# Folding w_out beside the logits, w2 of seven experts by row halves, and a reordered tail, in an attention and two-MoE kernel on one core

## The chip, the core and the metric

The kernel runs on one NeuronCore of a Trainium2 chip. The core has TensorE (matmuls; "PE" in the profile, its weight loads "PEld"), VectorE ("DVE"), ScalarE ("ACT"), GpSimd ("POOL"), SyncE ("SP", which here issues every DMA), and 16 DMA engines. TensorE's array can be split into strips of 32 columns or 32 rows: an operation whose output has 32 rows of PSUM uses one column strip (column group), and the profile writes its shape as 128*32. The metric is the device time of one execution in microseconds (us). Lower is better.

## What is computed

```python
x = local_global_attention(q_l, k_l, v_l, q_g, k_g, v_g)   # 2304 tokens, 512 features
silu = g * sigmoid(g);  g = x @ w_gate;  val = x @ w_val    # d_ff = 1536
x = (silu * val) @ w_out                                    # w_out: 1536 x 512

# soft MoE on that x: 32 slots, 8 experts with 4 slots each
logits = x @ phi                                            # 512 x 32
d = softmax(logits, axis=0);  c = softmax(logits, axis=1)
slot_input = (d.T @ x).reshape(8, 4, 512)
for e in range(8):
    slot_out[e] = relu(slot_input[e] @ w1[e]) @ w2[e]       # 512 x 1024, 1024 x 512
out = c @ slot_out                                          # 2304 x 512
```

The kernel never forms the second x. It uses logits = h @ (w_out @ phi), with h = silu * val, and puts w_out into the slot inputs at the end.

## The kernel before

The program is written in order by hand, and each engine runs its own instructions in that order. Instructions of one engine are never reordered by a scheduler.

**Attention** comes first (16 units). It leaves x transposed in 18 tiles of 128 tokens, kept in five blocks: blocks 0, 1, 2 (512 columns each) are the group G1, blocks 3 (384 columns, `BA`) and 4 (256 columns, `BB`) are G2.

**First MoE.** d_ff is cut into `NFC` = 12 chunks of 128. For G1 and each chunk c, `gate` and `val` run on each of the three blocks: 12 matmuls each (`mm3`, line 598: 4 pieces of the contraction, each as three products of rounded and remainder parts). ACT then takes tanh of the gate, DVE multiplies twice (lines 613 and 622) and transposes into `hT`. G2 does the same afterwards with weights fetched again from DRAM.

Between the matmuls other work is inserted by a hand-written plan. A step is one quarter of a `gate` or `val` (3 matmuls); `at(k, f)` runs f after step k. A chunk of G1 is `S1` = 24 steps and a chunk of G2 is `S2` = 16. In G1 that work is, for each chunk:

- `wprime(c)` makes wp[c] = w_out[chunk] @ phi (128 x 32) in three parts. Part a (step +9) transposes w_out on TensorE (`pwt`) and ACT copies it (`woT`). Part b (step +12), the fold, has four matmuls (`pwp`, line 642), one for each quarter of the 512 features, each in its own column strip; DVE copies the four partial sums (`ws`). Part e (step +15) adds the four with one matmul against a stack of four identities (`pws`, line 651), and ACT copies the result to `wp`.
- `logits_piece(0, [c - 1])` (step +5, line 669) adds chunk c-1's part of the logits: three matmuls, one for each block, in column strips 0, 1 and 2 of the tile `L`. They read the `u` tiles of chunk c-1. There are two pools of `u` tiles, for even and odd chunks, with three tiles each, so the tanh of chunk c+1 can write only when chunk c-1's tile has been read.

**Slot inputs.** `sums` (line 760) adds exp(logits).T @ h for a block in 32x32 tiles. For block `BA` it runs in three calls during the end of G2, and after the last of them `last_expert` issues the DMA of the last w1 (`ha`, 2 MB), which overwrites that block's `hT`. The steps here are counted from k = `begin(10, BB)`.

**Experts.** w2 of an expert is 1024 x 512 (2 MB) and is loaded in two halves of 1 MB. `w2_load` has two ways. A half by rows is a run of 8 KB for each partition and holds half of the contraction for all columns. A half by columns holds the whole contraction for 256 output columns, in runs of 1 KB. `order2` says which way and in what order: experts 0 to 5 by rows, then columns 0 to 255 of experts 6 and 7, then columns 256 to 511 of experts 6 and 7. `expert2(e, a)` (line 1194) adds expert e's part to output half a: 8 matmuls in four column strips, into `pso[a]`.

**Tail.** `slots_out(a)` copies `pso[a]` (ACT), spreads it with one matmul (`ps4`) and copies it again (DVE). `tiles_out(a, kk)` multiplies by c for 8, 8 and 2 tiles of tokens, copies the results out of PSUM (ACT and DVE in turn) and issues the output DMAs: 9 for each half of the columns, most of them of 256 KB.

An fp32 matmul shows as two records in the profile.

Of the kernel before, what the change touches and what calls it, by code (L numbers as in the profile page):

```python
# [23 lines left out]
NC = DM // P  # L24
# [21 lines left out]
def attention_moe_soft_moe_kernel(  # L46
# [15 lines left out]
    nc = tc.nc  # L62
    FF = w_gate.shape[1]
    NFC = FF // P
    NS = phi.shape[1]
    E, _, F2 = w1.shape
# [18 lines left out]
    istack = cpool.tile([P, NS], F32, name="istack")  # L85
# [3 lines left out]
    phi_sb = cpool.tile([P, NC, NS], F32, name="phi_sb")  # L89
# [4 lines left out]
    for i, (_, n) in enumerate(BLOCKS):  # L94
        pool = x2pool if i in GROUPS[-1] else x1pool
        t = pool.tile([P, 2 * NC * n * P], F32R, name=f"x{i}")
        t = t.rearrange("p (a c n) -> p a c n", a=2, c=NC)
# [169 lines left out]
    pw = ps_sc.tile([P, 512], F32, tag="sc", name="pw")  # L267
# [21 lines left out]
    for g in (0, 1, 3, 2):  # L289
# [7 lines left out]
        for r in range(3):  # L297
# [3 lines left out]
            k = window(first)[1]  # L301
# [283 lines left out]
    def at(k, f):  # L585
        plan.setdefault(k, []).append(f)
# [40 lines left out]
    def wprime(c):  # L627

        d = {}

        def a():
            pt = ps_w.tile([P, NC, P], F32, tag="wt", name=f"pwt{c}")
            for cc in range(NC):
                nc.tensor.transpose(pt[:, cc], wo[c][:, cc * P : cc * P + P], ident)
            wo.pop(c)
            t = d["t"] = wtmp.tile([P, NC, P], F32, tag="woT", name=f"woT{c}")
            nc.scalar.activation(t, pt, AF.Copy)  # L637

        def b():
            pp = ps_w.tile([P, P], F32, tag="wp", name=f"pwp{c}")  # L640
            for j in range(NC):
                nc.tensor.matmul(
                    pp[32 * j : 32 * j + 32], phi_sb[:, j], d["t"][:, j],
                    start=True, stop=True, skip_group_check=True,
                )
            d["s"] = wtmp.tile([P, P], F32, tag="ws", name=f"ws{c}")
            nc.vector.tensor_copy(d["s"], pp)

        def e():
            pw = ps_w.tile([P, NS], F32, tag="wp", name=f"pws{c}")  # L650
            nc.tensor.matmul(pw, d["s"], istack, start=True, stop=True)
            nc.scalar.activation(wp[c], pw, AF.Copy)

        return a, b, e

    def logits_piece(g, cs, blks=None):

        group = GROUPS[g]
        per = 4 // len(group)

        def f():
            if g not in Lps:
                Lps[g] = ps_L.tile([P, 512], F32, tag="L", name=f"L{g}")
            for c in cs:
                for bi, blk in enumerate(group):
                    if blk not in (blks or group):
                        continue
                    cg, n = bi * per + c % per, cols(blk)
                    nc.tensor.matmul(  # L669
                        Lps[g][32 * cg : 32 * cg + 32, :n], wp[c], us.pop((c, blk))[:, :n],  # L670
                        start=(c < per), stop=(c >= NFC - per), skip_group_check=True,
                    )

        return f
# [171 lines left out]
    S1, S2 = 2 * NC * len(G1), 2 * NC * len(G2)  # L846
    for c in range(NFC):

        if c > 0:
            at(S1 * c + 5, logits_piece(0, [c - 1]))  # L850
        for k, f in zip((9, 12, 15), wprime(c)):
            at(S1 * c + k + (5 if c == 0 else 0), f)
        if c + 2 >= NFC:
            w_fetch(c + 2)
        for bi, blk in enumerate(G1):
            if c + 1 < NFC:
                w_prep(3 * (c + 1) + bi)
            if c > 0:
                gate(0, c, blk)
            prep_some(2)  # L860
            val(0, c, blk)
            prep_some(3)
# [33 lines left out]

    HD = DM // 2
    w1s, w2h, slots = {}, {}, {}
    NWHOLE = E - 2
    order2 = [(e, a, True) for e in range(NWHOLE) for a in range(2)]  # L900
    order2 += [(e, a, False) for a in range(2) for e in range(NWHOLE, E)]

# [7 lines left out]
    t = epool[0].tile([P, 4096], F32, name="dr0", tag="e0")  # L910
    t = [t[:, 512 * k : 512 * k + 512] for k in range(5)]
    d0, a, b, top, turned, tokens, sums, NJ = part_end(0, t[0], (t[1], t[0], t[1]), t[2:])
# [16 lines left out]
    k = base + 30  # L929
# [25 lines left out]
    def first_done():  # L955

        t = place["x"] = x2pool.tile([P, 8 * cols(BA)], F32, name="xa", tag=f"x{BA}")
        w2_load(0, t)
        o = 8 * cols(BA) - cols(BB)
        place["rB"] = t[:, o:]  # L960
        Ls, r = t[:, o - 2 * cols(BA) : o - cols(BA)], t[:, o - cols(BA) : o]
        d, a, b, top, turned, tokens, sums, NJ = part_end(1, Ls, [Ls], [r])

        al = []

        def spread():
            b()
            top(0)
            al.append(weights(0))

        def merge(i):
            nc.vector.scalar_tensor_tensor(
                out=Ts[:, i], in0=d["T"][i][:, 0:NF], scalar=al[0][:, 1:2], in1=Ts[:, i],
                op0=ALU.mult, op1=ALU.add,
            )

        def aside(i):
            t = upools[1].tile([P, 512], F32, tag="u", name=f"TA{i}", bufs=3)
            nc.scalar.activation(t[:, :NF], d["T"][i][:, 0:NF], AF.Copy, scale=al[0][:, 1:2])
            place["T", i] = t[:, :NF]  # L980

        def last_expert():

            place["h"] = h2pool.tile([P, NFC * cols(BA)], F32, name="ha", tag=f"h{BA}")
            w1_load(E - 1, place["h"][:, 0:4096])

        place["merge"] = merge
        k = begin(10, BB)
        at(begin(9, BB) + 3, a)
        at(begin(9, BB) + 6, spread)  # L990
        at(k + 1, lambda: turned(0))
        at(k + 3, lambda: nc.scalar.activation(Ts, Ts, AF.Copy, scale=al[0][:, 0:1]))
        at(k + 5, tokens)
        at(k + 6, lambda: weighted(0, al[0], ds[:, 2, 0:1]))
        for i, j in enumerate(range(0, NJ, 4)):
            at(k + 7 + 2 * i, sums(j, min(j + 4, NJ)))
        at(k + 12, last_expert)
        for i in (2, 3):
            at(k + 10 + i, lambda i=i: aside(i))

    wot = []

# [6 lines left out]
    for c, blk in order:  # L1009
        if blk == BA:  # L1010
            i = NFC + c
# [23 lines left out]
    d, a, b, top, turned, tokens, sums, NJ = part_end(2, Ls, [Ls], [place["rB"]])  # L1035
# [43 lines left out]
    t = dpool.tile([P, 4 * NF], F32, tag="Ts", name="sT")  # L1079
    nc.gpsimd.memset(t[:, : 5 * E * DG], 0.0)  # L1080
    t = t[:, : 5 * E * DG].rearrange("p (c k) -> p c k", c=5)
# [6 lines left out]
    for c in range(NFC):  # L1088
        cg = c % 4
        for h, hs in enumerate((H1, H2)):  # L1090
            nc.tensor.matmul(
                psi[h][32 * cg : 32 * cg + 32], TT[:, c], wot[c // 4][:, c % 4, hs],
                start=(c < 4), stop=(c >= NFC - 4), skip_group_check=True,
# [5 lines left out]
    for c in range(NC):  # L1099
        nc.tensor.matmul(  # L1100
            psTi[:, c], si[c // 2][:, c % 2 * P : c % 2 * P + P], istack,
            start=True, stop=True, skip_group_check=True,
# [88 lines left out]
    def expert2(e, a):  # L1191
        for f in range(NF2):
            j = f % 4
            nc.tensor.matmul(  # L1194
                pso[a][32 * j : 32 * j + 32], hx[f][:, NS * e : NS * e + NS], w2h[e, a, f],
                start=(e == 0 and f < 4), stop=(e == E - 1 and f >= 4), skip_group_check=True,
            )

    def slots_out(a, beside=()):

        sb = upools[1].tile([P, HD], F32, tag="u", name=f"psb{a}", bufs=3)
        nc.scalar.activation(sb, pso[a], AF.Copy)
        for f in beside:
            f()
        ps4 = psT.tile([P, DM], F32, tag="t", name=f"ps4{a}")
        nc.tensor.matmul(ps4[:, :HD], rep4, sb, start=True, stop=True)
        nc.vector.tensor_copy(s4[:, a], ps4[:, :HD])
# [3 lines left out]
    def tiles_out(a, kk):  # L1211
        n, qs = (2, range(4)) if kk < 2 else (1, [3])
        po = {q: psT.tile([P, 2, HD], F32, tag="t", name=f"po{a}_{kk}_{q}") for q in qs}
        for i in range(n):
            for q in qs:
                r = slice(32 * q, 32 * q + 32)
                nc.tensor.matmul(  # L1217
                    po[q][:, i], cT[r, 2 * kk + i], s4[r, a],
                    start=True, stop=True, skip_group_check=True,
                )  # L1220
        cs = slice(a * HD, a * HD + HD)
        for q in qs:
            o = ob[nob[0] % len(ob)]
            nob[0] += 1
            if q % 2 == 0:
                nc.scalar.activation(o[:, :n], po[q][:, :n], AF.Copy)
            else:
                nc.vector.tensor_copy(o[:, :n], po[q][:, :n])
            if kk < 2:
                rs = slice(G + 2 * P * kk, G + 2 * P * kk + 2 * P)  # L1230
                nc.sync.dma_start(out_b[q, rs, cs].rearrange("(i p) f -> p i f", p=P), o)
            else:
                nc.sync.dma_start(out_b[:, 0:G, cs], o[:, 0])

    for e in range(E):
        expert2(e, 0)
    slots_out(0, [lambda: expert2(0, 1)])
    for e in range(1, E):
        expert2(e, 1)
        if e <= 3:  # L1240
            tiles_out(0, e - 1)
    slots_out(1)
    for kk in range(3):
        tiles_out(1, kk)
# [58 lines left out]
```

## Time and profile before

| | |
|---|---|
| Median of 3 runs | 533.63 us (532.14 to 534.77) |
| The profiled execution's own time | 531.98 us |
| Its span, first to last instruction | 529.6 us |
| Mean granted TensorE clock | 0.987 |
| TensorE busy | 494.8 us, 93% of the span |
| VectorE busy | 303.7 us, 57% |
| ScalarE busy | 182.2 us, 34% |
| Bytes moved by DMA | 109.93 MB, mean 208 GB/s |

The span is what the trace covers; the execution's own time has 2.4 us around it. The chain that ended last is 68% TensorE, 12% "issue" (the engine waited for nothing that the profile shows), 8% ScalarE and 7% DMA. The stretches of the trace are: attention to about 111 us, G1 from there to 346 us, G2 to 457 us, the end of the slot inputs to 471 us, expert first layers to 485 us, expert second layers and the output to the end. Busy shares are averages over these; a saving counts only where the stage is bound by what is saved.

### The profile page before, as it was taken

Reading aid. Unit: us, or ns where it says so; the run is one execution under the profiler, and the core shown is the slowest. Engines: PE = TensorE matmul, PEld = TensorE weight load, DVE = VectorE, ACT = ScalarE, POOL = GpSimd, SP = SyncE. Lnnn points to the kernel's source line nnn. Section 1 sums busy time; section 2 is a strip of 40 time slices with the busy share of each in tenths; the row PEclk is TensorE's granted clock in tenths of the full one; section 3 lists DMA queues with packets and bytes.
Section 4 is the critical chain, followed back from the end, with each engine's and each line's share of the span. In section 5 each row is a group of like instructions: output and inputs, shape, how many; then the busy total and the mean of one; then the engine's idle time right before and its main releaser. Section 6 shows DMA issues by size and latency. Waiting matters only on the chain.

```text
span 529.6 us, 12507 instructions
## 1 busy us (share of the span) xinstructions
PE 494.8 (93%) x5110; PEld 369.1 (70%) x5110; DVE 303.7 (57%) x801; ACT 182.2 (34%) x550; POOL 97.1 (18%) x137
## 2 busy tenths in 40 slices
PE   7779999999999999999999999999999999989592
PEld 4567888887777677777677777786599998434241
DVE  7558888767776667677677667353233434550022
ACT  5849898963323223223223223111111112210011
POOL 7854465421201001001001001000000000010000
PEclk9999999999999999999999999999999999999897
DMA  8997696503653444444444463223099996899965
GB/s 208 278 293 230 206 271 172 167 11 100 219 178 124 158 157 156 143 139 160 139 141 159 140 228 125 85 94 147 2 366 400 410 414 210 298 420 419 359 201 179
DMA packets 51169, 109.93 MB, mean 208 GB/s; under 512 B 3752, under 2 KB 35496, under 8 KB 47656
## 3 DMA queue, kind: packets, MB, share of 16 engines
q1 hardware_dynamic: 51112, 109.13, 61.0%
q8 instruction: 40, 0.66, 0.5%
q14 instruction: 17, 0.14, 0.1%
HBM read 88.93 MB, written 20.19 MB: 206 GB/s over the span
## 4 chain that ended last, share of the span: by engine, by line
PE 68%; issue 12%; ACT 8%; DMA 7%; DVE 3%; SPq 0%; DVEq 0%; ACTq 0%
PE pval L598 23%; PE pgate L598 22%; DMA f<-in_w_dram 4%; PE sc L342 4%; ACT p L363 3%; PE T L760 3%; PE o L386 3%; PE ppT L372 2%; DMA fw<-in_w_dram 2%; PE pso L1194 2%; PE L L669 2%; ACT woT L637 1%; PE po L1217 1%; DMA qT<-in_qT_dram 1%; PE gs L447 1%
## 5 line engine op out<-in xcount | busy, mean ns | idle before, releaser
L598 PE MATMUL pval<-x,w 128*128 128x512 f32 x432 | 112.2, 400 | 0.0
L598 PE MATMUL pgate<-x,w 128*128 128x512 f32 x432 | 109.7, 398 | 0.0
L598 PEld LDWEIGHTS pval<-x,w 128*128 128x128 f32 x432 | 79.3, 188 | 28.2 <-issue 11.6
L598 PEld LDWEIGHTS pgate<-x,w 128*128 128x128 f32 x432 | 79.4, 189 | 16.6
L613 DVE SCALAR_TENSOR_TENSOR u<-u,pgate 128x512 f32<-128x512 f32 (+2 forms) x60 | 36.4, 607 | 84.6 <-ACT u L612 84.5
L612 ACT ACTIVATE u<-pgate 128x512 f32<-128x512 f32 (+2 forms) x60 | 31.8, 530 | 128.1 <-PE pgate L598 106.3
L622 DVE SCALAR_TENSOR_TENSOR u<-u,pval 128x512 f32<-128x512 f32 (+2 forms) x60 | 36.4, 607 | 48.6 <-PE pval L598 48.5
L172 POOL TENSOR_TENSOR w<-wb,w 128x512 fp32r<-128x512 f32 x24 | 31.2, 1302 | 179.9 <-ACT w L171 179.8
L363 ACT ACTIVATE p<-sm,nm 128x128 f32<-128x128 f32 x128 | 49.4, 395 | 0.0
L598 PE MATMUL pgate<-x,wr 128*128 128x384 f32 (+1 forms) x288 | 49.3, 314 | 0.0
L598 PEld LDWEIGHTS pgate<-x,wr 128*128 128x128 f32 x288 | 43.5, 188 | 8.1 <-issue 7.4
L598 PE MATMUL pval<-x,wr 128*128 128x384 f32 (+1 forms) x288 | 48.4, 313 | 0.0
L598 PEld LDWEIGHTS pval<-x,wr 128*128 128x128 f32 x288 | 43.1, 188 | 7.0 <-issue 7.0
L171 ACT ACTIVATE w<-wb 128x512 fp32r<-128x512 f32 x24 | 15.2, 632 | 86.7 <-issue 51.3
L342 PE MATMUL sc<-kS,qB 128*64 128x128 f32 x512 | 35.3, 286 | 7.9 <-ACT pG L466 3.3
L342 PEld LDWEIGHTS sc<-kS,qB 128*64 128x64 f32 x512 | 29.5, 142 | 13.6 <-issue 8.5
L353 DVE CUSTOM_DVE_ANT_0 sm<-sc,masks 128x128 f32<-128x128 f32 x128 | 28.9, 287 | 10.6 <-PE sc L342 8.9
L157 DVE SCALAR_TENSOR_TENSOR wb<-wv,wb 128x512 f32<-128x512 f32 x36 | 25.2, 700 | 3.5
L1080 POOL MEMSET sT<- 128x1440 f32 x1 | 1.3, 1297 | 138.5 <-PE U L1055 138.5
L625 DVE STREAM_TRANSPOSE hT<-u 128x512 f32<-128x512 f32 x36 | 25.6, 712 | 1.3
L143 DVE SCALAR_TENSOR_TENSOR wb<-raw,wb 128x512 uint32<-128x512 uint32 x36 | 24.9, 692 | 1.1
L363 ACT ACTIVATION_READ_ACCUMULATOR p<-sm,nm 128x1 f32 x128 | 24.9, 195 | 0.0
(207 smaller groups left out, 667.8 us busy)
## 6 DMA issues: line engine op xcount, KB each, us to landing
e<-in_w_dram SPq DMA_DIRECT2D x7, 2048.0 KB, 12.4
w_d<-w SPq DMA_DIRECT2D x24, 512.0 KB, 2.6
wr<-w_d SPq DMA_DIRECT2D x12, 1024.0 KB, 6.1
f<-in_w_dram SPq DMA_DIRECT2D x10, 1024.0 KB, 14.7
raw<-in_wgate_dram SPq DMA_DIRECT2D x12, 512.0 KB, 3.5
raw<-in_wval_dram SPq DMA_DIRECT2D x12, 512.0 KB, 4.0
raw<-in_wout_dram SPq DMA_DIRECT2D x12, 512.0 KB, 3.5
kS<-in_kS_dram SPq DMA_DIRECT2D x7, 736.0 KB, 7.2
```

The source lines that it names most:

```text
L143: nc.vector.scalar_tensor_tensor(out=d["t"], in0=d["raw"][:, :, 0], scalar=29, in1=d["t"], op0=ALU.logical_shift_right, op1=ALU.bitwise_or,)
L157: nc.vector.scalar_tensor_tensor(out=w, in0=d["v"], scalar=F64_NORMAL, in1=w, op0=ALU.is_ge, op1=ALU.mult)
L172: nc.gpsimd.tensor_tensor(out=wl, in0=w, in1=wh, op=ALU.subtract)
L342: nc.tensor.matmul(sc[64 * (i % 2) : 64 * (i % 2) + 64, i // 2], qb[:, hp, blk], kS[n][:, hp, 32 * s0 : 32 * s0 + 128], start=True, stop=T ...
L353: nc.vector.tensor_tensor_reduce(out=sm[:, bp], in0=sc[:, bp], in1=masks[:, 4 * tp + bp], scale=-SCALE, scalar=3e38, op0=ALU.add, op1=ALU.min,
L363: nc.scalar.activation(d["p"][hp][:, bp], d["sm"][hp][:, bp], AF.Exp, bias=d["nm"][:, hp, bp : bp + 1], scale=-1.0, accum_out=d["rs"][:, b ...
L386: nc.tensor.matmul(o[32 * g : 32 * g + 32, bp, hp], d["pT", hp][:, bp, 32 * g : 32 * g + 32], vW[n % 2][k][:, m, 2 * h2 + hp], start=True, ...
L598: nc.tensor.matmul(ps[:, :n], w[:, 2 * k + a, cc * P : cc * P + P], xt[b][:, cc], start=(cc == 0 and i == 0), stop=(cc == NC - 1 and i == 2),)
L612: nc.scalar.activation(u[:, :n], pg[:, :n], AF.Tanh, scale=0.5)
L613: nc.vector.scalar_tensor_tensor(out=u[:, :n], in0=u[:, :n], scalar=1.0, in1=pg[:, :n], op0=ALU.add, op1=ALU.mult)
L622: nc.vector.scalar_tensor_tensor(out=u[:, :n], in0=u[:, :n], scalar=0.5, in1=pv[:, :n], op0=ALU.mult, op1=ALU.mult)
L625: nc.vector.transpose(out=hT[blk][:, c], in_=u[:, :n])
```

## The change

There are three edits.

**Fold.** Part a of `wprime` stays at step +9 (+14 for chunk 0). The four matmuls of part b now all write to one column strip, rows 96 to 127 of PSUM, and add up there, instead of to four strips. The copy takes 32 rows, and part e contracts over 32 rows instead of 128. Part b of chunk c moves to step +3 of the next chunk (step +13 of the same chunk for chunk 11) and is put right behind `logits_piece(0, [c - 1])`, which moves there from step +5 of chunk c, so it is 22 steps later for chunks up to 9. Part e follows 6 steps after part b, which is the step of the next chunk's part a.

**Slot sums.** The three `sums` calls of block `BA` move from steps k+7, k+9, k+11 to k+6, k+7, k+8; `last_expert` from k+12 to k+9; two copies (`aside`) from k+12, k+13 to k+10, k+11.

**Tail.** w2 of expert 6 is loaded by rows, so that only expert 7 is loaded by column halves. The order of `expert2` mixes second halves into the first halves. All of `tiles_out(0, ...)` comes behind `expert2(7, 1)`, and `slots_out(1)` behind that.

```diff
         def b():
+            r = slice(3 * NS, 4 * NS)
             pp = ps_w.tile([P, P], F32, tag="wp", name=f"pwp{c}")
             for j in range(NC):
                 nc.tensor.matmul(
-                    pp[32 * j : 32 * j + 32], phi_sb[:, j], d["t"][:, j],
-                    start=True, stop=True, skip_group_check=True,
+                    pp[r], phi_sb[:, j], d["t"][:, j],
+                    start=(j == 0), stop=(j == NC - 1), skip_group_check=True,
                 )
             d["s"] = wtmp.tile([P, P], F32, tag="ws", name=f"ws{c}")
-            nc.vector.tensor_copy(d["s"], pp)
+            nc.vector.tensor_copy(d["s"][r], pp[r])

         def e():
+            r = slice(3 * NS, 4 * NS)
             pw = ps_w.tile([P, NS], F32, tag="wp", name=f"pws{c}")
-            nc.tensor.matmul(pw, d["s"], istack, start=True, stop=True)
+            nc.tensor.matmul(pw, d["s"][r], istack[r], start=True, stop=True)
             nc.scalar.activation(wp[c], pw, AF.Copy)
...
+        last = c == NFC - 1
+        f, fold, back = wprime(c)
+        at(S1 * c + (14 if c == 0 else 9), f)
+        k = S1 * c + 13 if last else S1 * (c + 1) + 3
         if c > 0:
-            at(S1 * c + 5, logits_piece(0, [c - 1]))
-        for k, f in zip((9, 12, 15), wprime(c)):
-            at(S1 * c + k + (5 if c == 0 else 0), f)
+            at(k, logits_piece(0, [c - 1]))
+        at(k, fold)
+        at(k + 6, back)
...
-    NWHOLE = E - 2
+    NWHOLE = E - 1
...
         for i, j in enumerate(range(0, NJ, 4)):
-            at(k + 7 + 2 * i, sums(j, min(j + 4, NJ)))
-        at(k + 12, last_expert)
+            at(k + 6 + i, sums(j, min(j + 4, NJ)))
+        at(k + 9, last_expert)
         for i in (2, 3):
-            at(k + 10 + i, lambda i=i: aside(i))
+            at(k + 8 + i, lambda i=i: aside(i))
...
-    for e in range(E):
-        expert2(e, 0)
-    slots_out(0, [lambda: expert2(0, 1)])
-    for e in range(1, E):
-        expert2(e, 1)
-        if e <= 3:
-            tiles_out(0, e - 1)
+    for e, a in ((0, 0), (1, 0), (2, 0), (3, 0), (4, 0), (0, 1), (1, 1), (5, 0), (2, 1), (3, 1),
+                 (6, 0), (4, 1), (5, 1), (7, 0)):
+        expert2(e, a)
+    slots_out(0, [lambda: expert2(6, 1)])
+    expert2(7, 1)
+    for kk in range(3):
+        tiles_out(0, kk)
     slots_out(1)
```

## Rows read from the trace of the kernel before

**Rows 1.** Windows: stretch, length, busy us per engine (instructions), clock, DMA share, GB/s.

```profile
150.00:321.00 171.00, 169.36 (x816) 125.53 (x815) 118.13 (x194) 46.30 (x89) 23.21 (x18) 1.00 0.47 158
```

**Rows 2.** Timeline of TensorE in one chunk of G1: start, us, what.

```profile
210.64 2.95 PE L598 MATMUL pgate<-x,w 128*128 128x512 f32 x12
213.43 1.54 PE L598 MATMUL pval<-x,w 128*128 128x512 f32 x6
214.90 1.06 PE L669 MATMUL L<-u,wp 128*32 128x512 f32 x6
215.89 1.66 PE L598 MATMUL pval<-x,w 128*128 128x512 f32 x6
...
220.62 0.86 PE L598 MATMUL pval<-x,w 128*128 128x512 f32 x3
221.64 0.43 PE L642 MATMUL pwp<-woT,phi_sb 128*32 128x128 f32 x8 [0.16 <-ACT woT L637]
222.00 2.35 PE L598 MATMUL pval<-x,w 128*128 128x512 f32 x9
224.19 0.34 PE L651 MATMUL pws<-istack,ws 128*128 128x32 f32 x2
```

**Rows 3.** The tile woT over the whole trace: who waited for it (us, times).

```profile
  PEld pwp L642: 6.1, 10
```

**Rows 4.** Windows of the end, same columns as Rows 1.

```profile
454.00:458.00 4.00, 4.00 (x53) 2.35 (x52) 1.30 (x4) 1.43 (x3) 0.00 (x0) 1.00 0.44 124
458.00:492.00 34.00, 30.37 (x383) 13.94 (x382) 11.54 (x27) 4.35 (x10) 2.05 (x2) 1.00 1.01 420
492.00:504.00 12.00, 5.89 (x66) 2.11 (x64) 0.00 (x0) 0.38 (x1) 0.00 (x0) 0.77 1.08 349
506.00:508.50 2.50, 2.50 (x46) 1.15 (x34) 0.88 (x2) 0.93 (x2) 0.00 (x0) 1.00 0.00 1
509.00:515.00 6.00, 6.00 (x95) 3.08 (x90) 1.71 (x3) 1.09 (x2) 0.00 (x0) 1.00 1.01 330
516.00:518.50 2.50, 1.87 (x20) 1.09 (x18) 0.89 (x2) 0.50 (x2) 0.00 (x0) 1.00 0.20 57
```

**Rows 5.** Timeline of the DMA issues on SyncE: start, us, what.

```profile
455.63 0.38 SPq L906 DMA_DIRECT2D ha<-in_w_dram  x1
...
508.20 5.04 SPq L1231 DMA_DIRECT2D out_dram<-ob  x8
...
518.62 4.30 SPq L1231 DMA_DIRECT2D out_dram<-ob  x7
```

**Rows 6.** Timeline of TensorE in the tail.

```profile
497.68 0.42 PE L1194 MATMUL pso<-f,hb 128*32 128x256 f32 x3 [2.37 <-DMA f<-in_w_dram]
...
506.41 1.15 PE L1217 MATMUL po<-s,xa 32*128 32x256 f32 x16
```

**Rows 7.** The chain of work that ended last, in the tail.

```profile
500.70 3.64 PE pso L1194 x32
...
505.48 1.00 PE pso L1194 x16
```

**Rows 8.** Timeline of TensorE, 458 to 470 us.

```profile
459.27 1.98 PE L1027 MATMUL idle<-e,ident 128*128 128x512 f32 x4
...
466.16 2.85 PE L1091 MATMUL psi<-wo,TT 128*32 128x256 f32 x48 [0.68 <-DVE w L785]
```

**Rows 9.** The chain of work that ended last, in G2.

```profile
354.06 1.43 PE pval L598 x12
```

**Rows 10.** Timeline of TensorE around the slot sums of block BA.

```profile
450.95 0.94 PE L760 MATMUL T<-h,xa 32*32 32x384 f32 x32 [0.46 <-DVE Lr L742]
451.82 0.98 PE L598 MATMUL pgate<-x,wr 128*128 128x256 f32 x6
452.74 0.93 PE L760 MATMUL T<-h,xa 32*32 32x384 f32 x32
```

**Rows 11.** The page's costliest groups: busy us, mean ns | idle before, what ended it.

```profile
L613 DVE SCALAR_TENSOR_TENSOR u<-u,pgate 128x512 f32<-128x512 f32 (+2 forms) x60 | 36.4, 607 | 84.6 <-ACT u L612 84.5
```

## The prediction

> **What bounds the kernel now.** I read the profile stage by stage, since the three edits fall into three stages. First come the windows of the middle of G1: TensorE is busy 169.4 of 171 us there, VectorE 118.1, and the DMA engines at less than half [rows 1]. So in G1 whatever TensorE executes beside the gate and val matmuls, or waits for, is paid in full.
>
> Second, the timeline of one chunk says what that is. Twelve undisturbed matmuls take from 210.64 to 213.43, so one takes 0.2325 us, three 0.70, six 1.40, nine 2.09 [rows 2]. An interruption costs its own time plus what its neighbours lose. For the fold, `pwp`: the three matmuls ahead of it take 1.02 instead of 0.70, among that 0.16 of waiting for ACT's copy `woT`; the fold itself 0.36; the nine behind it 2.19 instead of 2.09. That is 0.32 + 0.36 + 0.10 = 0.78 us. The wait is there in 10 of 12 chunks [rows 3]. Without it the entry costs what it costs the logits, 1.47 - 1.40 = 0.07, and the fold 0.53. Over 12 chunks: 10 x 0.78 + 2 x 0.53 = 8.9 us.
>
> Third, the end. The windows show DMA at 44% from 454 to 458 us, then full until 504: at 420 GB/s while runs of 8 KB are loaded, at 349 GB/s for the four last loads by columns; then nothing from 506 to 508.5, full again with the first half's output, and 20% from 516 to 518.5 [rows 4]. The first outputs are issued at 508.20 and the second half's at 518.62 [rows 5]. So the end is a chain of DMA with two holes in it. TensorE meanwhile waits for loads [rows 6], and in part of that time it is granted half its clock: the mean is 0.77 from 492 to 504 [rows 4], and two `expert2` take 3.64 us there, where one takes 1.00 a little later at full clock [rows 7].
>
> **The fold beside the logits.** Removed are twelve folds, 8.9 us. Added are twelve folds in one column strip, eleven of them behind three logits matmuls that occupy the other three strips. Four matmuls are eight records of 128 columns. Four fp32 records of 512 columns that nothing overlaps take 1.98 us [rows 8], 0.495 each, so 0.124 for 128 columns and 0.99 for the fold. The logits take 215.89 - 214.90 = 0.99 [rows 2]. If the strips run on their own, the fold ends with them and costs nothing beyond them. I take 0.05 each for a later start, 0.55 for eleven. Both ends: 0, and 0.99 each if the fold runs behind the logits.
>
> Do strips run on their own when the program names one strip several times in a row? That is the question of this edit, and `psi` answers it: its loop issues two fp32 matmuls (four records) to one strip, then two to the next. Its 48 records of 256 columns take 2.85 us [rows 8]. One by one they would take 48 x 0.248 = 11.9. That is all four strips at once, so I take the overlap. The Trainium skill, "TensorE: Matmul & The Clock Gate" (Part 3: Packing small matmuls), says the contrary: matmuls start and end strictly in program order, without reordering, and only weight loads are pulled ahead. By that rule `psi` would overlap hardly more than the ends of neighbouring groups, so the trace disagrees with it; what it would make of this change is the second rival.
>
> Chunk 0's fold has no logits beside it: 0.99 + 0.07 + 0.10 = 1.16 us.
>
> **Part e over 32 rows.** The trace has no such matmul among these, so I bound it. In G2 twelve matmuls of 256 columns take 1.43 us [rows 9], six 0.715. Between two `sums`, which use 32-row tiles, six take 452.74 - 451.82 = 0.92 [rows 10]: 0.20 for one leaving and one entering, 0.10 each. Before, part e entered free, the nine matmuls ahead of it having no loss beyond the fold's. Now it may pay 0.10 to enter and 0.10 to leave for the transposes, and saves a return to the big matmuls of its own. Bounds are -0.1 and +0.2; the nearest row is the one entry, so +0.1 for each of twelve: +1.2 us. The Trainium skill, "TensorEngine Tiling (Array Packing)" (Tiling Modes, Key Properties), says that changing the tiling mode drains the engine. It speaks against this part of the edit and gives no figure; the rows' 0.10 us agrees with a short drain, and the sum stays as it is.
>
> **Costed at nothing.** VectorE's copy `ws` keeps 128 columns, so its time, and VectorE is 69% busy [rows 1]. The logits now stand right behind `gate` of block 0, and that gate's tanh may write its `u` only when they have read the old one, about 1.0 us later than before. Behind tanh on ACT stand a weight preparation's first operation, and on VectorE the multiplication, which waits for tanh already, 84.5 us over 60 [rows 11]. What hides it: TensorE goes on with the next two blocks' worth of matmuls, 2 x 2.79 us [rows 2], before it needs that gate's PSUM tile again (there are three). Without that cover it would cost 1.0 us or more in each of ten chunks.
>
> G1 together: -8.9 + 0.55 + 1.16 + 1.2 = **-6.0 us**; between -8.9 + 1.16 - 1.2 = -8.9 at best and -8.9 + 11 x 0.3 + 1.16 + 2.4 = -2.0, where 0.3 stands for a fold that overlaps two thirds.
>
> **Sums sooner.** The first `sums` waited 0.46 us for VectorE's transpose `Lr` [rows 10], whose step does not move; a step sooner it waits longer, and three matmuls (0.36) that covered it come after it. TensorE's chain loses 0.36. But the last call stands three steps, 9 x 0.119 = 1.07 us, sooner, and the DMA `ha`, issued at 455.63 [rows 5] on the end of that call, goes out that much sooner. No queue is passed: on SP it still stands between the second and third load of `wo`. DMA has idle time there and is full behind it [rows 4], so what is gained is carried to the last load. Bounds 0 (if a later load is then issued too late) and 1.1; I take 1.0.
>
> **Tail.** Expert 6's two loads go at 420 instead of 349 GB/s: 1.05 MB takes 2.50 instead of 3.00 us, so 1.0 us less. TensorE's waits end at 497.68 and 500.70 [rows 6, 7], 3.02 apart, as the slower rate says. Expert 7's first half was the last but two of the loads, the others landing at about 503.7 and 506.7. Now: first half at 500.7 + 3.0 - 1.0 - 1.0 = 501.7, last load at 504.7.
>
> From first half to the first output matmul `po` at 506.41 [rows 6] were 5.7 us, with three `expert2` and one spreading matmul. Now again three `expert2` (7 first, 6 second, 7 second half) and the spreading. As slow as before, `po` starts at 501.7 + 5.7 = 507.4. At full clock 2 x 0.82 us go [rows 7], so 505.7, which is also last load plus one `expert2`, 504.7 + 1.0. In either case all output matmuls follow without another `expert2` among them.
>
> The first output DMA went out 1.8 us after `po`. A half is 2304 x 256 x 4 bytes = 2.36 MB, 7.1 us at 330 GB/s [rows 4]. The second half's can now follow the first half's data directly, 7.1 us instead of 10.4 behind its first issue (518.62 - 508.20); its copies run meanwhile on ACT and VectorE, idle then. From 518.62 to the span's end were 11.0. So the end is `po` + 1.8 + 7.1 + 11.0 = 525.6 to 527.3, against 529.6: -4.0 to -2.3. The trace does not say which clock there will be (second halves now fill part of the waits), so I take **-3.2 us**.
>
> **Sum.** -6.0 - 3.2 = -9.2 us. Against the profiled execution (span 529.6, its own time 531.98) that is 522.8; the median shown is 533.63, 1.65 above it, so 524.4.
>
> **The rivals.** (1) The tail gains little. For: if the clock falls as before, the second halves of experts 4 and 5, now ahead of expert 7's first, take 1.82 us each [rows 7]; expert 6's row load lands at 498.7, its rest takes 0.9, so TensorE reaches expert 7 at 503.2 instead of 501.7 and `po` is at 508.9: -0.8 us. Total -6.8: 526.8. Against: those halves also keep TensorE busy.
>
> (2) The folds run behind the logits: 11 x 0.99 = 10.9 instead of 0.55. G1 gives -8.9 + 10.9 + 1.16 + 1.2 = +4.4; with the tail +1.2: 534.8. `psi` speaks against it. The rule on strict order in the Trainium skill, "TensorE: Matmul & The Clock Gate" (Part 3: Packing small matmuls), would lead here.
>
> (3) Slower: tanh held by the logits. If TensorE had to stand until logits (0.99) and multiplication (0.61 [rows 11]) are through, that is 1.6 us in ten chunks, +16: 540.4. It decides from 1.2 us a chunk. The spare PSUM tiles speak against it.
>
> **How the numbers follow.** Forecast 0.67, rival 1 0.20, rival 2 0.08, rival 3 0.05. A measurement here tells 0.5% (2.7 us) from no change. Forecast and rival 1 are faster: 0.87; rival 2 is within 0.5%: 0.08; rival 3 slower: 0.05. The range goes from the best fold with the best tail, -8.9 - 4.0 = -12.9, where I stop at -12.6, to a part-overlapped fold with the middle tail, -2.0 - 3.2 = -5.2: 521.0 to 528.4, which holds rival 1.
>
> **What would show it.** In the profile after: eight `pwp` records spread over the time of the six `L` records, and nothing of `pwp` behind them; a chunk of G1 shorter by 0.55 to 0.7 us; no wait of `pwp` for `woT`; `sums` waiting about 0.8 us for `Lr`; `ha` issued 1.1 us earlier relative to the end of G2; two loads by columns instead of four; DMA without a hole between the two output halves. Wrong it would be with `pwp` starting when `L` has ended, with gate matmuls waiting for PSUM, or with `po` starting more than 1 us later relative to the load of `ha` than before.

## The result and the profile after

The changed kernel took 526.88 us in the median (525.68 to 528.46, 4 runs) against 533.01 us (4 runs): ratio 0.9883, 95% interval 0.9845 to 0.9921. A second measurement with more runs of both (6 and 23) gave 526.9 against 533.84, ratio 0.9857 (0.9821 to 0.9893). So it is 1.2 to 1.4% faster, 6 to 7 us. The forecast was 524.4, which is 9.2 us less than before, with a range of 521.0 to 528.4. The direction and the range held; the gain is a quarter to a third smaller than forecast. The measured time stands next to that of rival 1 (526.8), but what rival 1 describes did not happen, as shown below, so that agreement is chance.

The profiled execution has a span of 524.97 us, 4.7 less than before. To see where that comes from, the span is cut at three marks that every trace shows: the first gate matmul, the first matmul on weights fetched again (start of G2), and the end of the last gate or val matmul.

| | before | after |
|---|---|---|
| first gate matmul starts at | 110.89 | 113.72 |
| G1 lasts | 234.93 | 229.47 |
| G2 lasts | 111.22 | 111.58 |
| start of G2 to end of the span | 183.83 | 181.77 |

So the two edited stages gained 5.46 + 2.06 = 7.5 us, and the attention, in which not one instruction changed, was 2.8 us later in this execution. The experiments show how much of such a difference is chance.

One chunk of G1 in the changed kernel, timeline of TensorE:

```profile
212.89 0.63 PE L672 MATMUL L<-u,wp 128*32 128x512 f32 x3
212.91 0.62 PE L644 MATMUL pwp<-woT,phi_sb 128*32 128x128 f32 x4
213.35 0.61 PE L672 MATMUL L<-u,wp 128*32 128x512 f32 x3
213.38 0.60 PE L644 MATMUL pwp<-woT,phi_sb 128*32 128x128 f32 x4
213.91 3.06 PE L598 MATMUL pval<-x,w 128*128 128x512 f32 x12
216.81 1.55 PE L598 MATMUL pgate<-x,w 128*128 128x512 f32 x6
218.29 0.40 PE L654 MATMUL pws<-istack,ws 32*128 32x32 f32 x2
218.63 0.66 PE L634 MATMUL pwt<-ident,wb 128*128 128x128 f32 x4
219.04 1.64 PE L598 MATMUL pgate<-x,w 128*128 128x512 f32 x6
220.52 1.79 PE L598 MATMUL pval<-x,w 128*128 128x512 f32 x7
```

Compare with [rows 2]. Four of the fold's records run while the first three records of the logits do, and four with the second three. The pair takes 213.91 - 212.89 = 1.02 us; the logits alone took 0.99. The fold, 0.78 us of this chunk before, now costs 0.03. No matmul waits for `woT` any more.

The windows of the same stretch as [rows 1], and of the end, as in [rows 4]:

```profile
150.00:321.00 171.00, 171.00 (x839) 135.72 (x838) 122.32 (x200) 46.63 (x92) 23.57 (x19) 1.00 0.47 159
...
454.00:492.00 38.00, 34.39 (x436) 16.91 (x438) 12.65 (x30) 4.35 (x10) 2.05 (x2) 1.00 1.00 412
495.00:501.00 6.00, 4.17 (x48) 2.29 (x52) 0.00 (x0) 0.00 (x0) 0.00 (x0) 0.73 1.01 329
502.00:505.90 3.90, 3.73 (x48) 1.94 (x40) 0.95 (x2) 0.76 (x3) 0.00 (x0) 1.00 0.02 5
507.00:512.50 5.50, 4.13 (x40) 2.74 (x36) 3.33 (x6) 2.45 (x5) 0.00 (x0) 1.00 1.03 340
513.00:514.00 1.00, 0.71 (x4) 0.27 (x2) 1.00 (x2) 0.98 (x2) 0.00 (x0) 1.00 0.46 54
515.00:520.00 5.00, 0.00 (x0) 0.00 (x0) 0.00 (x0) 0.00 (x0) 0.00 (x0) 0.50 1.05 351
520.50:522.50 2.00, 0.00 (x0) 0.00 (x0) 0.00 (x0) 0.00 (x0) 0.00 (x0) 0.50 0.27 75
```

TensorE has no idle time left in this stretch of G1. At the end, the hole between the two output halves has shrunk from over 2.5 us to about 1 us (513 to 514), and the last 2 us of data run at a DMA share of 0.27.

The DMA issues at the end, as in [rows 5]:

```profile
449.86 0.33 SPq L1015 DMA_DIRECT2D wo<-wo_d  x1
452.30 0.38 SPq L915 DMA_DIRECT2D ha<-in_w_dram  x1
...
505.95 5.03 SPq L1240 DMA_DIRECT2D out_dram<-ob  x8
511.07 0.69 SPq L1242 DMA_DIRECT2D out_dram<-ob  x1
511.86 6.27 SPq L1240 DMA_DIRECT2D out_dram<-ob  x7
```

The second half's first output is issued 5.9 us behind the first half's, where it was 10.4 [rows 5].

### The profile page after: what moved, and what is told of

Same layout as the page of the kernel before. It is cut to its first block, busy times and chain, and to the rows that moved or that the text cites. A ratio compares the mean times of both kernels' runs of the same rounds, so it can differ in the third digit from the quotient of the medians.

```text
span 525.0 us, 12516 instructions
## 1 busy us (share of the span) xinstructions
PE 493.2 (94%) x5110; PEld 380.8 (73%) x5110; DVE 307.1 (58%) x801; ACT 181.3 (35%) x550; POOL 97.0 (18%) x137
## 4 chain that ended last, share of the span: by engine, by line
PE 79%; DMA 7%; ACT 5%; DVE 4%; issue 2%; SPq 1%; DVEq 0%; ACTq 0%
PE pval L598 28%; PE pgate L598 27%; DMA f<-in_w_dram 4%; PE sc L342 4%; PE T L763 3%; PE ppT L372 2%; PE o L386 2%; ACT p L363 2%; PE L L672 2%; DMA fw<-in_w_dram 2%; PE pwp L644 2%; PE pwt L634 1%; PE pso L1203 1%; DVE sm L353 1%; PE gs L447 1%
## 5 line engine op out<-in xcount | busy, mean ns | idle before, releaser
L598 PE MATMUL pval<-x,w 128*128 128x512 f32 x432 | 107.1, 397 | 0.0
L143 DVE SCALAR_TENSOR_TENSOR wb<-raw,wb 128x512 uint32<-128x512 uint32 x36 | 25.4, 706 | 1.1
L149 DVE SCALAR_TENSOR_TENSOR wb<-raw,wb 128x512 uint32<-128x512 uint32 x36 | 25.1, 696 | 0.0
```

The lines of the kernel that those rows point to most:

```text
L143: nc.vector.scalar_tensor_tensor(out=d["t"], in0=d["raw"][:, :, 0], scalar=29, in1=d["t"], op0=ALU.logical_shift_right, op1=ALU.bitwise_or,)
L149: nc.vector.scalar_tensor_tensor(out=d["t"], in0=d["raw"][:, :, 1], scalar=0xC0000000, in1=d["t"], op0=ALU.bitwise_and, op1=ALU.bitwise_or,)
L598: nc.tensor.matmul(ps[:, :n], w[:, 2 * k + a, cc * P : cc * P + P], xt[b][:, cc], start=(cc == 0 and i == 0), stop=(cc == NC - 1 and i == 2),)
```

## The experiments

All of them were measured against the kernel before. In the table times are in us, read from the profiles at the marks above; the last four columns count from the start of G2. "Before" and "after" are the first profiles of each. The five kernels from "fold apart" to "rows, old order" ran once each (535.66, 520.21, 524.44, 525.19 and 538.21 us), so only their traces are compared.

| kernel | first gate | G1 | G2 | `ha` issued | last w2 load landed | first output issued | end of span |
|---|---|---|---|---|---|---|---|
| before | 110.89 | 234.93 | 111.22 | 109.81 | 160.75 | 162.38 | 183.83 |
| after | 113.72 | 229.47 | 111.58 | 109.10 | 159.45 | 162.76 | 181.77 |
| after again | 115.09 | 229.43 | 111.59 | 109.11 | 159.45 | 162.28 | 181.39 |
| fold only | 113.08 | 229.43 | 111.24 | 109.83 | 160.69 | 162.31 | 183.82 |
| tail only | 112.56 | 234.94 | 111.21 | 109.80 | 159.87 | 162.70 | 181.66 |
| sums only | 113.31 | 235.06 | 111.57 | 109.09 | 161.47 | 162.84 | 184.37 |
| fold apart | 109.27 | 242.74 | 112.09 | 109.61 | 160.02 | 162.85 | 181.74 |
| part e over 128 rows | 110.95 | 226.02 | 111.58 | 109.10 | 159.80 | 162.63 | 181.26 |
| sums at 7, 8, 9 | 112.06 | 229.43 | 111.23 | 109.10 | 159.39 | 162.22 | 181.08 |
| narrow output first | 113.67 | 229.47 | 111.59 | 109.11 | 159.68 | 161.91 | 180.12 |
| rows, old order | 115.55 | 235.11 | 111.21 | 109.80 | 159.75 | 163.78 | 185.35 |
| together | 111.47 | 226.02 | 111.22 | 109.10 | 159.54 | 161.76 | 180.13 |

**After again**: the changed kernel with no edit.

> The changed kernel once more. Its first profile has a stretch of 6.8 us in the attention at half the clock, and its first gate matmul starts at 113.7 us instead of 110.9, although nothing of the attention was changed. Theory A (chance): the clock falls there in some executions and not in others; then this profile has another start of the first gate, and without a low stretch it is about 110.9 and the span about 522. Theory B (the change itself makes the attention slower, for instance by where the program lies in memory): first gate at 113.7 again. Both: G1 229.5 us, G2 111.6 us, from the end of G2 to the span's end 70.2 us.

Ratio 0.9857 (0.9821 to 0.9893). G1, G2 and the end are as in the first profile within 0.4 us, the first gate is 1.4 us later. Theory B falls: the first gate starts anywhere from 109.27 to 115.55 in the twelve profiles, and in the three kernels without the fold's edit (tail only, sums only, rows with old order) at 112.56, 113.31 and 115.55. But theory A falls too in what it said about the clock: "narrow output first" had no stretch of low clock in the attention and yet began its first gate at 113.67. So the start of the first gate moves from execution to execution, as the time does (the 23 runs of the kernel before go from 531.24 to 537.06 us), and the clock is not all of it.

**Fold only**, the edit of `wprime` and of its steps as in the diff, nothing else.

> The kernel before with the fold's edit alone. Theory A: G1 takes 229.5 us instead of 234.9, G2 and the end are as before, so 5.4 us less in the median, about 527.6, ratio 0.990. Theory B (the change slows the attention): 2.8 us of that are lost again, 530.4, ratio 0.995, and the profile shows the first gate at 113.7.

Ratio 0.9885 (0.9855 to 0.9914), 527.48 us. G1 is 229.43, 5.5 us shorter; everything behind it is as before within 0.1 us. The fold's gain stands by itself and reaches the end in full.

**Tail only**, `NWHOLE` and the order at the end as in the diff.

> The kernel before with the tail's edit alone (expert 6 by rows, the new order of the second layers). If the tail's gain stands by itself: last load 1.0 us sooner after the end of G2, first output about 1 to 2 us sooner after that end, span 2.0 to 2.4 us shorter, ratio 0.996. If it needs the earlier slot sums: only half of it.

Ratio 0.9953 (0.9928 to 0.9979). Last load 0.88 us sooner, end 2.17 us sooner. The tail's gain does not need the sums' edit: with it the end is at 181.77 and 181.39, without it at 181.66. The expected first output, 1 to 2 us sooner, did not come: it is issued at 162.70, 0.3 us later than before. The gain lies behind it, where the second half's first output now follows after 6.6 us instead of 10.4.

**Sums only**, the three `sums`, `last_expert` and `aside` as in the diff.

> The kernel before with the slot sums' edit alone. The prediction's step says that the last load lands 1.0 us sooner. The rival: the second load of wo, which waits for the val of (10, BB), is issued about 1.6 us later, because the sums now come ahead of that val's last matmuls; then ha queues behind it, the last load lands 0.3 to 0.4 us sooner, and the time is the same, ratio 0.999 to 1.000. Both: TensorE loses 0.4 us at the first sums.

Ratio 1.0011 (0.9982 to 1.004). `ha` goes out 0.72 us sooner, G2 takes 0.35 us longer, no load of w2 lands sooner (the last but one 157.86 against 157.85, the last 161.47 against 160.75), and the end is 0.5 us later. The edit gains nothing when it is alone. The second load of `wo` was indeed issued 1.95 us later; whether that is the reason is tried below.

**Fold apart**: each fold three matmuls behind the logits.

```diff
-        at(k, fold)
+        at(k + 1, fold)
```

> The changed kernel, but each fold three gate or val matmuls (one step) behind the logits instead of directly behind them. If the fold's gain is its overlap with the logits in the other column strips: the fold pays its 0.99 us and its own entry and exit again, 1.2 us as chunk 0's did, in eleven chunks, so G1 is 229.4 + 11 x 1.2 = 242.5 us. Rival (the gain came from the waits for woT that are gone, not from the overlap): G1 stays within 2 us of 229.4. End of the kernel as in the changed one.

G1 is 242.74 us. The timeline of TensorE shows what is paid:

```profile
212.30 1.06 PE L672 MATMUL L<-u,wp 128*32 128x512 f32 x6
213.29 0.97 PE L598 MATMUL pval<-x,w 128*128 128x512 f32 x3
214.18 1.06 PE L644 MATMUL pwp<-woT,phi_sb 128*32 128x128 f32 x8
215.17 2.37 PE L598 MATMUL pval<-x,w 128*128 128x512 f32 x9
```

Eight records in one strip take 0.99 us when they are alone. With the same four matmuls in one strip, the same late step and no wait for `woT`, the change would have made G1 7.8 us slower than before. So the change gains nothing without the overlap with the logits: 13.3 us of G1, 1.2 in each of eleven chunks, hang on the fold standing directly behind them. A late fold that keeps its four strips, and so loses only the wait for `woT`, was not run; what that alone would have gained is not shown.

**Part e over 128 rows**: the copied sums lie in one tile whose other 96 rows are zeroed once, and part e contracts over all 128 rows again.

```diff
-            d["s"] = wtmp.tile([P, P], F32, tag="ws", name=f"ws{c}")
+            d["s"] = ws0
             nc.vector.tensor_copy(d["s"][r], pp[r])
...
-            r = slice(3 * NS, 4 * NS)
-            nc.tensor.matmul(pw, d["s"][r], istack[r], start=True, stop=True)
+            nc.tensor.matmul(pw, d["s"], istack, start=True, stop=True)
...
+    ws0 = wtmp.tile([P, P], F32, tag="ws", name="ws0")
+    nc.gpsimd.memset(ws0, 0.0)
```

> The changed kernel, but part e contracts over 128 rows again: the copied sums stand in rows 96 to 127 of one tile whose other rows are zeroed once. If the use of 32-row tiles is what makes part e with the transposes cost 0.92 us instead of 0.69, and the last part e alone 0.54 instead of 0.22: G1 is 11 x 0.23 + 0.3 = 2.8 us shorter, 226.6. Rival (what costs is that part e's matmul stands directly ahead of the transposes, whatever its rows): G1 stays at 229.4. A wait of part e on the zeroing or on the copy would show as a wait of pws.

G1 is 226.02, 3.4 us shorter than after. Timeline of TensorE:

```profile
212.91 1.55 PE L598 MATMUL pgate<-x,w 128*128 128x512 f32 x6
214.30 0.30 PE L653 MATMUL pws<-istack,ws 128*128 128x32 f32 x2
214.44 0.64 PE L634 MATMUL pwt<-ident,wb 128*128 128x128 f32 x4
214.83 1.63 PE L598 MATMUL pgate<-x,w 128*128 128x512 f32 x6
```

From the first of the six gate matmuls to `pws` are now 1.39 us, no loss, where the changed kernel has 1.48; and `pws` keeps the engine 0.14 us, where it has 0.34. Both together are 0.29 us in each of twelve chunks, 3.5 us, which is what G1 lost. It is the 32 rows that cost, not the place ahead of the transposes.

**Sums at 7, 8, 9**: one step later than in the change, so behind the last matmuls of (10, BB).

```diff
-            at(k + 6 + i, sums(j, min(j + 4, NJ)))
-        at(k + 9, last_expert)
+            at(k + 7 + i, sums(j, min(j + 4, NJ)))
+        at(k + 10, last_expert)
```

> The changed kernel with the three sums one step later (k+7, k+8, k+9; ha at k+10). If the second load of wo is what the earlier first sums hold up: that load is issued 104.7 us after the start of G2 again instead of 106.7, ha at about 109.1, the same as in the changed kernel, G2 takes 111.2 instead of 111.6, and the last load lands 0.4 us sooner or more (159.0 after the start of G2 instead of 159.45). Rival (ha alone sets the loads): the last load lands where it did, 159.45.

`wo` is issued 104.72 us after the start of G2 again, G2 takes 111.23, and `ha` goes out at 109.10 as in the changed kernel. The last load lands at 159.39, only 0.06 sooner. So the late `wo` did not hold up the loads. The later first `sums` give TensorE back 0.35 us of G2, and `ha` is as early as with all three steps: two of the three bring all that the change brought.

**Narrow output first**: in each half the 128 KB transfer of the global tokens goes out first.

```diff
-    for kk in range(3):
+    for kk in (2, 0, 1):
         tiles_out(0, kk)
     slots_out(1)
-    for kk in range(3):
+    for kk in (2, 0, 1):
         tiles_out(1, kk)
```

> The changed kernel, but in each output half the 128 KB transfer of the global tokens goes out first instead of last. In the last 1.5 us of data of the changed kernel the DMA share is 0.25, as if that transfer ran on 4 of 16 engines, and between the halves the share falls to 0.3 for 1 us. If that transfer's few engines set the end: the end is 1.0 to 1.5 us sooner behind the first output's issue (17.5 to 18.0 us instead of 19.0), and the hole is gone. Rival (latency of the last issue, or SyncE's issue times, set it): 19.0 as before.

From the first output's issue to the end are 18.2 us instead of 19.0, a little less gain than expected, and the end is 1.3 or 1.65 us sooner, by the two profiles of the changed kernel. The first output is now the narrow one and goes out 1.18 us behind the first `po` instead of 1.78, so part of the gain is an earlier start; the two parts were not separated. Its windows:

```profile
506.25:507.00 0.75, 0.75 (x13) 0.63 (x10) 0.15 (x2) 0.06 (x1) 0.00 (x0) 1.00 0.22 40
...
513.00:514.00 1.00, 1.00 (x11) 1.00 (x12) 0.69 (x1) 0.30 (x1) 0.00 (x0) 0.50 0.84 263
514.00:515.00 1.00, 1.00 (x12) 0.68 (x4) 0.03 (x1) 0.38 (x1) 0.00 (x0) 0.50 0.43 81
...
521.00:522.00 1.00, 0.00 (x0) 0.00 (x0) 0.00 (x0) 0.00 (x0) 0.00 (x0) 0.50 0.23 78
```

At 506.25 the first data of the output is under way, that of the narrow transfer, and the share is 0.22: as if it ran on 4 of 16 engines. The hole between the halves is not gone, as was expected; it stands 1 us later (0.43 from 514 to 515, against 0.46 from 513 to 514), in a stretch in which TensorE is granted half its clock (0.50), so the two holes are not alike. The end at a low share has shrunk from 2 us to 1. That last us at 0.23 is not explained by the narrow transfer, which now goes first, and need not be: in the kernel before, the last load of w2, with no output under way yet, ends at a like share:

```profile
504.80:505.80 1.00, 1.00 (x10) 0.29 (x12) 0.28 (x1) 0.00 (x0) 0.00 (x0) 0.73 0.21 70
```

**Rows, old order**: the kernel before with `NWHOLE = E - 1` alone.

> The kernel before with expert 6's w2 by rows, everything else as before, also the old order of the second layers. If the tail's gain lies in the order (the output halves close up) and not in the faster loads: the last load lands 1.0 us sooner (159.8 after the start of G2 instead of 160.75), but expert 7's first half, on which the first outputs wait, is now the last load but one and lands 2.0 us later (156.9), so the first output goes out 2 us later, at 164.4, and the end is 185.8 after the start of G2 instead of 183.8. Rival (the 1.0 us of faster loads carries to the end by itself): 182.8.

The last load lands 1.0 us sooner and the end is 1.5 us later, 185.35. Faster loads alone are a loss: expert 7's first half comes one load later (it lands at 156.85 instead of 154.84) and the first outputs wait for it. The order is what turns the tail into a gain.

**Together**: part e over 128 rows, sums at 7, 8, 9, narrow output first.

> The changed kernel with three of the findings together: part e over 128 rows with zeroed rows, the sums at k+7, k+8, k+9, and the 128 KB output transfer first in each half. From the single runs: G1 226.0, G2 111.2, the end 180.0 after the start of G2. With the attention between 109.3 and 115.1 us as in the runs so far, 112 us in the middle, the span is 518 and the time 520, ratio to before 0.974, against 0.986 for the changed kernel. If the gains do not add (the loads, not the outputs, set the end then): the end stays at 181, ratio 0.976.

Ratio 0.9793 (0.9752 to 0.9833), 522.5 us, the lowest median of the kernels that ran more than once. In the trace G1 (226.02), G2 (111.22) and the end (180.13) are as expected, though the end is no sooner than with "narrow output first" alone. The ratio is 0.005 short of what was expected from these, with runs from 517.95 to 524.89; the attention, which the edits do not touch, spreads as widely.

## Why the prediction was right, and where it was too high

**The fold's overlap** was right. It was the question on which the gain hung, and `psi` [rows 8] had answered it: 0.05 us was taken for a fold beside the logits, 0.03 was measured. Rival 2 is shown wrong by the trace after, and "fold apart" gives its price. The rule of strict order in the Trainium skill, "TensorE: Matmul & The Clock Gate" (Part 3: Packing small matmuls), does not hold here, if records are issued in the order of the source: half of the fold's records, which stand behind all of the logits there, start before the logits' second three records (212.91 against 213.35).

**Part e** was mis-sized. The step took +0.1 us for each of twelve, within -0.1 and +0.2, from what it costs `sums` to enter 32-row tiles. Part e and the transposes `pwt` stood apart before. This is the rest of the chunk of [rows 2]:

```profile
217.39 1.56 PE L598 MATMUL pgate<-x,w 128*128 128x512 f32 x6
218.79 0.60 PE L634 MATMUL pwt<-ident,wb 128*128 128x128 f32 x4
219.15 1.63 PE L598 MATMUL pgate<-x,w 128*128 128x512 f32 x6
...
224.36 3.04 PE L598 MATMUL pgate<-x,w 128*128 128x512 f32 x12
227.24 2.94 PE L598 MATMUL pval<-x,w 128*128 128x512 f32 x12
```

With what their neighbours lose, the transposes cost 0.43 us and part e 0.26, together 0.69; in the changed kernel they cost 0.92. That is +0.23 for each chunk, over the bound, and some +2.8 us in G1 instead of +1.2. "Part e over 128 rows" gives the price of the 32 rows alone: 0.29 us, 3.5 us in G1. The entry was as expected (1.48 - 1.39 = 0.09 us). What the bound left out is that the engine is kept longer behind it: 0.34 us from `pws` to the transposes, against 0.14 over 128 rows.

Still G1 came out at -5.5 instead of -6.0, and that is partly luck. From one chunk's logits to the next chunk's were 19.30 to 19.41 us before; after, they are 18.84 to 18.87 in two of three chunks, but 18.58 or 18.59 in the third. Why the third gains 0.27 us more is open. The tanh that the logits now hold costs nothing, as argued: TensorE is busy 171.00 of 171 us in the middle of G1. Rival 3 did not occur.

**Sums sooner** was mis-sized, and in proportion this is the step that failed most. TensorE's loss was right: the wait for `Lr` grew from 0.46 to 0.82 us.

```profile
448.34 0.94 PE L763 MATMUL T<-h,xa 32*32 32x384 f32 x32 [0.82 <-DVE Lr L745]
449.21 0.62 PE L598 MATMUL pval<-x,wr 128*128 128x256 f32 x3
449.76 0.93 PE L763 MATMUL T<-h,xa 32*32 32x384 f32 x32
```

But that same 0.36 us also delays the last `sums` and with it `ha`. I subtracted it from TensorE's chain and not from the 1.07 us of `ha`, which is 0.71 sooner. And of that only 0.42 us arrives at the last load (159.87 with the tail only, 159.45 with both); alone the edit moved no load of w2. The late load of `wo` is ruled out as the reason. The bound of zero that the prediction had kept, a later load issued too late, is what the traces show: the loads `fw` wait for TensorE's `psi`, which is not sooner. The first goes out 121.87 us after the start of G2, against 121.50 with the tail only, and the DMA engines run short of work before its data come. Here are two us from 123 us after the start of G2, of "after" and then of "tail only":

```profile
466.20:467.20 1.00, 0.53 (x12) 0.05 (x3) 0.36 (x1) 0.38 (x1) 0.00 (x0) 1.00 0.88 295
467.20:468.20 1.00, 0.82 (x8) 0.82 (x8) 0.12 (x1) 0.10 (x1) 0.00 (x0) 1.00 0.91 336
...
470.50:471.50 1.00, 0.35 (x6) 0.18 (x2) 0.48 (x1) 0.47 (x1) 0.00 (x0) 1.00 1.06 442
471.50:472.50 1.00, 0.90 (x8) 0.78 (x8) 0.00 (x0) 0.00 (x0) 0.00 (x0) 1.00 0.96 393
```

The sum of the shares is 0.23 us lower, which is most of the 0.28 us between `ha` (0.70) and the last load (0.42). Why the edit alone moves no load of w2 at all is not settled.

**The tail's other steps** were nearly right. The loads by rows gave 0.9 of 1.0 us. From the landing of expert 7's first half (499.73) to the first `po`, 4.06 to 5.7 us were given, the first for the full clock:

```profile
504.17 1.56 PE L1226 MATMUL po<-s,xa 32*128 32x256 f32 x18
505.98 2.05 PE L1226 MATMUL po<-s,xa 32*128 32x256 f32 x16 [0.25 <-ACT ob L1235]
```

That is 4.44 us, and its first 1.4 us fall into a stretch of 3.4 us at half clock (0.50 from 497.7 to 501.1). The second profile of the same kernel had no such stretch there, nor had the six other kernels with this order, and all seven took 3.95 or 3.96 us. So rival 1, in which the clock eats the gain, did not occur; the clock cost 0.5 us in one of eight profiles. Then 18.1 us were given from first output to the end, and 19.0 and 19.1 measured. The step "the second half's can now follow the first half's data directly" left 0.9 us out: the hole is smaller, but not gone, and each half ends with a transfer of 128 KB that runs on few engines. With "narrow output first" 1.4 or 1.5 us less pass from the first `po` to the end, 0.6 of them before the first output is issued. The Trainium skill, "DMA: Bandwidth & Descriptors" (Why a DMA increments its semaphore by 16 and not by 1, How many engines), says that the number of engines is the largest, up to 16, that divides the slowest dimension of both sides. On the DRAM side that dimension is 4 here (4 batches), and the DMA share of 0.22 with this transfer alone under way agrees with 4 of 16. Nothing in the prediction had looked at it, though the trace before ends in the same way as the changed one:

```profile
526.00:527.50 1.50, 0.00 (x0) 0.00 (x0) 0.00 (x0) 0.00 (x0) 0.00 (x0) 0.50 0.21 48
```

So the tail, with 2.06 and 2.44 us in the two profiles, fell short of the given 3.2 by 1.1 and 0.8. The sums explain 0.6 of that, the loads by rows 0.1, and the way from the first output to the end 0.9 and 1.0; the way from first half to `po`, taken in the middle at 4.9 us and measured at 4.44 and 3.95, gave 0.5 and 0.9 back.

**The signs that the prediction named** held for the most part: `pwp` spread over `L`, no wait for `woT`, a chunk shorter by 0.58 us on average, 0.82 us of waiting for `Lr`, `ha` 1.07 us sooner relative to the end of G2. Two did not. The DMA still has a hole between the output halves. And `po` starts 51.87 us behind the issue of `ha` where it started 50.78 behind it before, 1.09 us later, which the prediction called a sign of being wrong (the second profile has 51.38, 0.60 later). That sign was badly chosen: with `ha` 1.07 us sooner and `po` at 505.7 to 507.4 instead of 506.41, the forecast itself puts `po` 0.4 to 2.1 us later relative to `ha`.

**The rest of the difference** between 9.2 and the measured 6 to 7 us is within the noise. The edited stages gained 7.5 and 7.9 us in the two profiles, and the interval of the second measurement is 5.7 to 9.6 us. The attention, which the edits do not touch, moves single executions by more than that difference; the profile before has the second earliest first gate of all twelve, so the 4.7 us between the two first spans say less than the stages do.

## What to carry to other kernels

Small fp32 matmuls that use one column strip can be put behind others that leave this strip free, and cost next to nothing (0.03 us here); but they must stand directly there, and a contraction cut down to 32 rows can cost more than the zeros it avoids. In a tail that is bound by transfers, look first at which load the first output waits for and at the DMA share of the last transfers. A wait that an edit adds must be subtracted from everything that the same edit moves forward on that engine.

## What the runs showed of the hardware that was not expected

Behind the same attention instructions, the first gate starts anywhere in a range of 6.3 us (109.27 to 115.55 in twelve profiles). Stretches of 3.4 or 6.8 us at half clock inside it stand in most of them, in the profile after at 36.9 us. But four profiles had none between 11 us and the first gate, and they spread from 110.89 to 113.67; and the earliest of all, 109.27, had one of 3.4 us. What else moves it is open; it was not tried.

G1, which is bound by TensorE, repeats far better: it took 229.43 to 229.47 us in the five profiles in which it is the changed kernel's, and 234.93 to 235.11 in the four in which it is that of the kernel before.
